# Attention over two head pairs at a time, in seven units of 128 keys, in place of four chunks of 112 keys for each pair

## The chip, the cores and the metric

The kernel runs on one core of one Trainium2 chip. The metric is the device time of one execution in microseconds; three runs of the kernel before gave 884.6, 885.2 and 886.6 us, so the median is 885.2 us.

## What is computed

The reference has three parts, one behind the other:

```python
# q, k, v: (4, 12, 448, 64)
scores = scale * q @ k.T - log(448)
attn   = 1 / (1 + exp(-scores))          # a sigmoid for each score, no sum over a row
x      = (attn @ v) -> (1792, 768)       # 4 batches of 448 tokens, 12 heads of 64
logits = x @ w_gate                      # 8 experts; each takes 224 tokens, the best logits first
x      = expert(x)                       # relu(x @ w1[e]) @ w2[e]
g      = s * relu(x @ w_in) ** 2 + b
out    = g @ w_out
```

Since the sigmoid has no sum over a row, each key contributes by itself: scores of some keys against all 448 queries, the sigmoid, and a product with those keys' rows of v that is added to the output.

## The kernel before

**Layout.** Two heads of 64 make a pair of 128 partitions; there are 4 batches of 6 pairs, 24 in all (`pairs`). Of each pair the kernel loads q and k, transposed, as 128 x 448 each (`load_qk`, L271), and v as 112 x 4 x 128 (`load_v`, L266).

**Scores.** `scores(n, c0, c1)` (L287) takes chunks of 112 keys of pair n. For a chunk the two heads j sit on the lower and the upper 64 rows of TensorE, each writes 112 keys x 448 queries to a PSUM bank of its own, and ScalarE makes one sigmoid of both (L304). From the third pair on q and k are split into a high part and a rest (`split_qk`, L278, on VectorE), and each head's product is made of three fp32r matmuls; the first two pairs (`PLAIN`) use fp32 matmuls on the raw tiles, which show as two instructions each in the trace. Three PSUM tiles (`psc`) of two banks each go round.

**Values.** `values(i)` (L308) multiplies the four chunks' sigmoids by v in fp32: the two heads sit on the two halves of 64 columns of TensorE, over 112 rows of keys, and add up in one bank `pv`. ScalarE copies the bank to `xT` (L321).

**Gate.** The logits of a batch are made from `xT`: `gate` (L323) puts pairs on four strips of 32 columns, four pairs first and the other two an iteration later; `gate_copy` takes them to SBUF, `gate_turn` (L335) turns them in an iteration of the next batch, and `prefs` (L348) makes ranks of them. The last batch leaves its last pair to `gate_last` (L343). `bracket` (L359) finds limits of the logits for the auction that follows.

**Order.** The order of work is written out by hand. Iteration i over the 24 pairs issues on SyncE's queue the loads of q and k of pair i+4 and of v of pair i+3; on VectorE the split of pair i+3; on TensorE values(i), the last two chunks of pair i+1 and the first two of pair i+2; then the gate's share. Each iteration ends with `CONV[i]` calls of `convert` (L159): VectorE turns one block of `w_in` or `w_out` from 8-byte words into floats in four or five instructions, SyncE's queue writes the block before out (`cv_out`, 384 KB) and then, when the raw tile is free, loads another (`cv_in`, 768 KB). SyncE's queue takes these in order, so a `cv_in` that waits for VectorE holds back the loads behind it. The raw q and k tiles have four buffers, the splits five and four (`wsp`, `wlp`).

After the loop come the transposes of `xT`, the auction, the gathers of tokens, the experts and the two layers; the change doesn't touch them.

Of the kernel before, what the change touches and what calls it, by code (L numbers as in the profile page):

```python
# [43 lines left out]
CONV = [1] * 8 + [2] + [1] * 7 + [2] + [1] * 5 + [0]  # L44
LATE = 8
PLAIN = 2
# [17 lines left out]
def tile_kernel(ctx, tc, qT, kT, v, wg, w1, w2, wi, wo, s2, b2, cst, out):  # L64
# [56 lines left out]
    qk = att.enter_context(tc.tile_pool(name="qk", bufs=4))  # L121
# [141 lines left out]
    raw_qk, two_qk, vt, attn, plg, lgs, pts = {}, {}, {}, {}, {}, {}, {}  # L263
# [14 lines left out]
    def split_qk(i):  # L278
        r = raw_qk.pop(i)
# [7 lines left out]
    def scores(n, c0, c1):  # L287
        if n >= len(pairs):
            return
        if c0 == 0:  # L290
            attn[n] = at.tile([CP, 2, NC, S], F32, name="attn")
        if n < PLAIN:
            terms = [(raw_qk[n], raw_qk[n])]
        else:
            h, lo = two_qk[n]
            terms = [(h, h), (lo, h), (h, lo)]
        for c in range(c0, c1):
            p = ps_s.tile([CP, 2, 512], F32, name="psc")
            for m, (kx, qx) in enumerate(terms):
                for j in range(2):  # L300
                    me = slice(j * D, (j + 1) * D)
                    T.matmul(p[:, j, :S], kx[me, 1, c * CP:(c + 1) * CP], qx[me, 0], start=(m == 0),  # L302
                             stop=(m == len(terms) - 1))
            A.activation(attn[n][:, :, c, :], p[:, :, :S], AF.Sigmoid, bias=nls[:CP], scale=1.0 / math.sqrt(D))  # L304
        if c1 == NC:
            (raw_qk if n < PLAIN else two_qk).pop(n)

    def values(i):  # L308
        a, v = attn.pop(i), vt.pop(i)
        pv = ps_v.tile([128, 512], F32, name="pv")  # L310
        for c in range(NC):
            for j in range(2):
                T.matmul(pv[j * 64:(j + 1) * 64, :S], v[:, c, j * D:(j + 1) * D], a[:, j, c, :],  # L313
                         start=(c == 0), stop=(c == NC - 1))
        b, p = pairs[i]
        xt = xT[:, p, b * S:(b + 1) * S]
        if i == len(pairs) - 1:
            A.copy(xt[:, :2 * CP], pv[:, :2 * CP])
            A.copy(xt[:, 2 * CP:], pv[:, 2 * CP:S])
        else:  # L320
            A.copy(xt, pv[:, :S])  # L321

    def gate(b, p0, p1, last):  # L323
        if p0 == 0:
            plg[b] = ps_l.tile([128, 512], F32, name="small")
# [9 lines left out]
    def gate_turn(b, stop):  # L335
        lg = lgs.pop(b)
        pt = ps_l.tile([128, 512], F32, name="small")
# [5 lines left out]
    def gate_last(b):  # L343
        for c in range(NC):
            T.matmul(pts[b][:, c], xT[:, NP - 1, b * S + c * CP:b * S + (c + 1) * CP], wgs[:, NP - 1, :E],
                     start=False, stop=(c == NC - 1))

    def prefs(b):  # L348
        V.tensor_copy(L[:, b * NC:(b + 1) * NC], pts.pop(b))
# [9 lines left out]
    def bracket(stage):  # L359
# [4 lines left out]
        elif stage == 1:  # L364
            pm = ps_l.tile([128, 512], F32, name="small")
            T.transpose(pm[:2, :CP], mm[:CP], ident[:CP, :CP])
            m2 = ep.tile([2, 1], F32, name="m2")
            V.tensor_reduce(m2, pm[:2, :CP], axis=AX.X, op=ALU.max)
            V.tensor_scalar(dg, ident[:2, :2], m2, None, op0=ALU.mult)
        else:  # L370
            pr = ps_l.tile([128, 512], F32, name="small")
            T.matmul(pr[:, :2], on[:2], dg, start=True, stop=True)
            V.tensor_copy(mm, pr[:, :2])
# [17 lines left out]
    keep_clock(WARM[0], ps_s.tile([CP, 2, 512], F32, name="psc")[:, 0])  # L391
# [4 lines left out]
    load_v(0)  # L396
    load_qk(1)
    nc.sync.dma_start(ct, cst)
    G.memset(wgs, 0.0)
    nc.sync.dma_start(wgs[:, :, :E], wg)  # L400
    load_v(1)
    load_qk(2)
    cv_in()
    load_qk(3)
    load_v(2)
    cv_in()
    cv_in()
    split_qk(2)
# [885 lines left out]
```

## Time and profile before

| | |
|---|---|
| median of three runs | 885.2 us |
| the profiled execution | 886.49 us, of it 884.7 us span |
| TensorE busy | 868.4 us (98%) |
| VectorE, ScalarE, GpSimd busy | 643.7, 520.1, 91.6 us |
| attention, from the first values to the last | 9.69 to 158.02 us |
| granted clock, mean | 0.993 |

Times within the profile are microseconds from the start of the span. "PE" is TensorE's matmuls, "PEld" its weight loads, "DVE" VectorE, "ACT" ScalarE, "POOL" GpSimd, "SPq" SyncE's queue of DMA issues. A matmul's end is modelled, so the spacing of starts tells more than the durations.

### The profile page before, as it was taken

The numbers are of one execution on the slowest core, as the hardware profiler recorded it, in microseconds if no ns is written. First come the engines' busy times: TensorE is split into PE (matmuls) and PEld (weight loads), VectorE is DVE, ScalarE is ACT, GpSimd is POOL, SyncE is SP. The second block draws the span as 40 slices with busy tenths as digits, with TensorE's granted clock in tenths as the row PEclk, the third lists the DMA queues.
The fourth block names the chain that finished last, engine by engine and source line by source line (L and its number), as shares of the span: only waits on it lengthen the run. The fifth ranks groups of instructions, "written<-read, shape, count | busy, mean of one in ns | idle before, by whom it ended". The sixth has DMA issues, their size and how long they took to land.

```text
span 884.7 us, 14248 instructions
## 1 busy us (share of the span) xinstructions
PE 868.4 (98%) x5226; PEld 749.3 (85%) x5226; DVE 643.7 (73%) x1114; ACT 520.1 (59%) x893; POOL 91.6 (10%) x150
## 2 busy tenths in 40 slices
PE   9999999889999999999999999999999999999997
PEld 4454544559999999999999999999998899999997
DVE  3987878556878677779778876867887666857681
ACT  6676767745765566643665546767766554645540
POOL 1000001323000000000255422000000000000003
PEclk9999999989999999999999999999999999999999
DMA  8989996666668686658899987675753333332313
GB/s 294 317 294 326 319 343 225 192 202 221 197 218 292 230 287 211 207 189 294 283 336 321 301 228 245 214 226 182 232 161 116 111 104 106 119 108 90 99 37 134
DMA packets 78122, 190.40 MB, mean 215 GB/s; under 512 B 9312, under 2 KB 31328, under 8 KB 77792
## 3 DMA queue, kind: packets, MB, share of 16 engines
q1 hardware_dynamic: 70144, 164.28, 56.6%
q0 software_dynamic: 7904, 25.17, 10.0%
q8 instruction: 42, 0.69, 0.3%
q14 instruction: 32, 0.26, 0.1%
HBM read 161.11 MB, written 42.47 MB: 230 GB/s over the span
## 4 chain that ended last, share of the span: by engine, by line
PE 94%; DVE 2%; ACT 1%; issue 1%; DMA 1%; POOL 0%; POOLq 0%; DVEq 0%; ACTq 0%
PE acc L727 16%; PE pv L313 9%; PE psc L302 8%; PE acc L728 8%; PE acc L1042 7%; PE acc L1039 7%; PE acc L1041 6%; PE acc L884 4%; PE acc L886 4%; PE acc L885 4%; PE acc L1148 4%; PE acc L1150 4%; PE acc L1149 4%; PE acc L753 1%; PE acc L754 1%; PE acc L755 1%
## 5 line engine op out<-in xcount | busy, mean ns | idle before, releaser
L244 ACT CAST wh<-raw 128x768 fp32r<-128x768 f32 (+1 forms) x248 | 201.2, 823 | 91.3 <-issue 68.1
L254 DVE TENSOR_TENSOR wl<-raw,wh 128x768 fp32r<-128x768 f32 (+1 forms) x244 | 225.8, 937 | 18.3 <-PE acc L1041 11.3
L727 PE MATMUL acc<-u,wh 128*128 128x448 f32 x384 | 120.8, 374 | 0.0
L728 PE MATMUL acc<-u,wl 128*128 128x224 f32 x384 | 101.6, 265 | 0.1
L727 PE MATMUL acc<-x,wh 128*128 128x448 f32 x288 | 94.8, 384 | 0.8 <-DVE x L721 0.8
L304 ACT ACTIVATE attn<-psc,nls 112x896 f32<-112x896 f32 x96 | 88.8, 1009 | 9.8 <-PE psc L302 9.8
L313 PE MATMUL pv<-attn,vt 112*64 112x448 f32 x384 | 77.5, 545 | 0.0
L728 PE MATMUL acc<-x,wl 128*128 128x224 f32 x288 | 76.8, 267 | 0.0
L727 PEld LDWEIGHTS acc<-u,wh 128*128 128x128 f32 x384 | 72.0, 188 | 5.3
L728 PEld LDWEIGHTS acc<-u,wl 128*128 128x128 f32 x384 | 73.3, 191 | 0.4 <-DVE wl L254 0.4
L884 PE MATMUL acc<-y,wh 128*128 128x448 f32 x192 | 70.9, 369 | 0.0
L886 PE MATMUL acc<-y,wl 128*128 128x448 f32 x192 | 70.2, 366 | 0.0
L885 PE MATMUL acc<-y,wh 128*128 128x448 f32 x192 | 70.2, 366 | 0.0
L313 PEld LDWEIGHTS pv<-attn,vt 112*64 112x64 f32 x384 | 25.4, 136 | 42.9 <-issue 36.1
L732 ACT COPY tmp<-acc 128x224 f32<-128x224 f32 x96 | 32.9, 343 | 48.7 <-PE acc L728 48.0
L727 PEld LDWEIGHTS acc<-x,wh 128*128 128x128 f32 x288 | 54.9, 191 | 4.9 <-issue 0.9
L1042 PE MATMUL acc<-wh,as 128*128 128x384 f32 x168 | 56.1, 334 | 0.0
L1041 PE MATMUL acc<-wl,as 128*128 128x384 f32 x168 | 56.1, 334 | 0.0
L1039 PE MATMUL acc<-wh,as 128*128 128x384 f32 x168 | 56.1, 334 | 0.0
L728 PEld LDWEIGHTS acc<-x,wl 128*128 128x128 f32 x288 | 55.7, 194 | 0.0
L733 DVE TENSOR_TENSOR tmp<-acc,tmp 128x224 f32<-128x224 f32 x78 | 30.1, 385 | 26.6 <-ACT tmp L732 26.1
L618 POOL DMA_INDIRECT xr<-xs,idx x16 | 16.6, 1036 | 264.4 <-PE px L718 252.1
(336 smaller groups left out, 1987.3 us busy)
## 6 DMA issues: line engine op xcount, KB each, us to landing
raw<-in_w_dram SPq DMA_DIRECT2D x128, 384.0 KB, 3.8
raw<-nw SPq DMA_DIRECT2D x64, 384.0 KB, 3.6
craw<-in_wi_dram SPq DMA_DIRECT2D x16, 768.0 KB, 7.1
raw<-mx SPq DMA_DIRECT2D x32, 384.0 KB, 5.0
nw<-co SPq DMA_DIRECT2D x24, 384.0 KB, 6.9
craw<-in_wo_dram SPq DMA_DIRECT2D x8, 768.0 KB, 6.4
ra<-in_wo_dram SPq DMA_DIRECT2D x8, 768.0 KB, 5.8
hs<-nw POOLq DMA_DIRECT2D x16, 384.0 KB, 9.6
```

What stands on the lines that cost most here:

```text
L244: A.copy(h, r)
L254: eng.tensor_sub(lo, r, h.bitcast(F32))
L304: A.activation(attn[n][:, :, c, :], p[:, :, :S], AF.Sigmoid, bias=nls[:CP], scale=1.0 / math.sqrt(D))
L313: T.matmul(pv[j * 64:(j + 1) * 64, :S], v[:, c, j * D:(j + 1) * D], a[:, j, c, :], start=(c == 0), stop=(c == NC - 1))
L727: T.matmul(p[:, :2 * CAP], wh, src[:, k].rearrange("p a s -> p (a s)"), start=(k == 0), stop=False)
L728: T.matmul(p[:, :CAP], wl, src[:, k, 0], start=False, stop=(k == n - 1))
L884: T.matmul(p, wh, src[:, k, 0], start=first, stop=False)
L885: T.matmul(p, wh, src[:, k, 1], start=False, stop=False)
L886: T.matmul(p, wl, src[:, k, 0], start=False, stop=last)
L1039: T.matmul(acc, hi, wh[:, cols], start=(opens[j] and u == 0 and c == 0), stop=False, skip_group_check=True)
L1041: T.matmul(acc, hi, wl[:, cols], start=False, stop=False, skip_group_check=True)
L1042: T.matmul(acc, lo, wh[:, cols], start=False, stop=(u == 3 and c == 1), skip_group_check=True)
```

## The change

Two neighbouring pairs, 2q and 2q+1, are taken together, in 12 steps (`NQ`). Of each pair's 448 keys the first 384 (`HD`) make three units of 128 keys; the 64 keys that are left of both pairs make one more unit, so there are seven: units 0 to 2 are the first pair's, 3 the two rests, 4 to 6 the second pair's. In unit 3 the scores of pair n go to the partitions n*64 to n*64+63, so that head j and pair n take the quarter of TensorE with row half j and column half n; it is made in plain fp32 from the raw tiles. In the values of unit 3 pair n is on row half n and head j on column half j, and the results end in the two banks of the two pairs. A step has two halves: values of units 0 to 2, then scores of the next step's units 0 to 2; values of units 3 to 6, then scores of the next step's units 3 to 6. v comes in one load for two pairs, 128 x 7 x 128. The raw tiles get five buffers and are held until unit 3 has used them. The gate's own PSUM bank goes; small results take tiles of the `psc` ring, and copies of them are ScalarE's. `gate` takes six pairs at once in the next batch's first step, and the last batch leaves two pairs to `gate_last`. `CONV` has a second 2 at one place less.

```diff
-CONV = [1] * 8 + [2] + [1] * 7 + [2] + [1] * 5 + [0]
+CONV = [1] * 8 + [2] + [1] * 14 + [0]
-PLAIN = 2
+PLAIN = 1
+NQ = B * NP // 2
+HD = 3 * 128
-    qk = att.enter_context(tc.tile_pool(name="qk", bufs=4))
+    qk = att.enter_context(tc.tile_pool(name="qk", bufs=5))
-    ps_v = att.enter_context(tc.tile_pool(name="ps_v", bufs=1, space=PSUM))
-    ps_l = att.enter_context(tc.tile_pool(name="ps_l", bufs=1, space=PSUM))
+    ps_v = att.enter_context(tc.tile_pool(name="ps_v", bufs=2, space=PSUM))
-    def load_v(i):
-        b, p = pairs[i]
-        vt[i] = vp.tile([CP, NC, 128], F32, name="vt", bufs=5)
-        nc.sync.dma_start(vt[i], v[b, p])
+    def load_v(q):
+        vt[q] = vp.tile([128, 7, 128], F32, name="vt", bufs=3)
+        nc.sync.dma_start(vt[q], v[q // 3, q % 3])
+    def small_psum():
+        return ps_s.tile([128, 2, 512], F32, name="psc")[:, 0]
+    def scores(q, units):
+        if q >= NQ:
             return
+        for r in units:
+            p = ps_s.tile([128, 2, 512], F32, name="psc")
+            if r == 3:
+                work = [(2 * q + n, slice(HD, S), slice(n * 64, n * 64 + 64)) for n in range(2)]
+            else:
+                c = r % 4
+                work = [(2 * q + r // 4, slice(c * 128, (c + 1) * 128), slice(0, 128))]
+            plain = q < PLAIN or r == 3
+            n_terms = 1 if plain else 3
+            for m in range(n_terms):
                 for j in range(2):
                     me = slice(j * D, (j + 1) * D)
+                    for n, keys, rows in work:
+                        if plain:
+                            kx = qx = raw_qk[n]
+                        else:
+                            h, lo = two_qk[n]
+                            kx, qx = ((h, h), (lo, h), (h, lo))[m]
+                        T.matmul(p[rows, j, :S], kx[me, 1, keys], qx[me, 0], start=(m == 0),
+                                 stop=(m == n_terms - 1), skip_group_check=True)
+            attn[q, r] = at.tile([128, 2, S], F32, name="attn", bufs=7)
+            A.activation(attn[q, r], p[:, :, :S], AF.Sigmoid, bias=nls, scale=1.0 / math.sqrt(D))
+    def values(q, block):
+        v = vt[q]
+        pvs[q, block] = pv = ps_v.tile([128, 512], F32, name="pv")
+        if block:
+            a = attn.pop((q, 3))
+            for n in range(2):
+                rows = slice(n * 64, n * 64 + 64)
+                for j in range(2):
+                    T.matmul(pvs[q, n][j * 64:(j + 1) * 64, :S], v[rows, 3, j * D:(j + 1) * D], a[rows, j],
+                             start=(n == 1), stop=(n == 0), skip_group_check=True)
+            done(q, 0)
+        for c in range(3):
+            a = attn.pop((q, 4 * block + c))
             for j in range(2):
+                T.matmul(pv[j * 64:(j + 1) * 64, :S], v[:, 4 * block + c, j * D:(j + 1) * D], a[:, j],
+                         start=(block == 0 and c == 0), stop=(block == 1 and c == 2), skip_group_check=True)
+        if block:
+            done(q, 1)
     def gate_last(b):
+        for p in (NP - 2, NP - 1):
+            for c in range(NC):
+                T.matmul(pts[b][:, c], xT[:, p, ...], wgs[:, p, :E],
+                         start=False, stop=(p == NP - 1 and c == NC - 1))
...
+    scores(0, range(7))
+    load_qk(4)
...
+    split_qk(2)
+    split_qk(3)
+    for q in range(NQ):
+        b, t = divmod(q, 3)
+        closing = b == B - 1
+        for n in (2 * q + 5, 2 * q + 6):
+            if n < 2 * NQ:
+                load_qk(n)
+        if q + 2 < NQ:
+            load_v(q + 2)
+        for half in range(2):
+            if q + 2 < NQ:
+                split_qk(2 * q + 4 + half)
+            values(q, half)
+            if t == 0 and b:
+                if half:
+                    gate_turn(b - 1, True)
+                    prefs(b - 1)
+                else:
+                    gate(b - 1, 0, NP, NP)
+                    gate_copy(b - 1)
+            if closing and (t == 1 or t + half == 1):
+                bracket(2 * t + half - 1)
+            if closing and t == 2 and not half:
+                gate(b, 0, NP - 2, NP - 2)
                 gate_copy(b)
+            scores(q + 1, range(3, 7) if half else range(3))
+            n = 2 * (NQ - q) - half
+            if 2 < n <= 6:
+                w_dma()
+            for _ in range({4: 1, 3: 1, 2: 2}.get(n, 0)):
+                w_high()
+                w_low(G)
+            for _ in range(CONV[2 * q + half]):
                 convert()
```

## Rows read from the trace of the kernel before

**Rows 1.** The page: the chain that ended last, by line.

```profile
PE acc L727 16%; PE pv L313 9%; PE psc L302 8%; PE acc L728 8%; PE acc L1042 7%; PE acc L1039 7%; PE acc L1041 6%; PE acc L884 4%; PE acc L886 4%; PE acc L885 4%; PE acc L1148 4%; PE acc L1150 4%; PE acc L1149 4%; PE acc L753 1%; PE acc L754 1%; PE acc L755 1%
```

**Rows 2.** Windows of attention: busy by engine (instructions), clock, DMA share, GB/s.

```profile
20.00:140.00 120.00, 120.00 (x818) 60.36 (x816) 99.28 (x145) 81.41 (x98) 0.00 (x0) 1.00 0.94 317
```

**Rows 3.** Timeline of TensorE over one iteration: start, duration, what, instructions merged.

```profile
27.62 3.23 PE L313 MATMUL pv<-attn,vt 112*64 112x448 f32 x16
30.78 0.46 PE L302 MATMUL psc<-wh 64*112 64x448 f32 x2
31.07 0.37 PE L302 MATMUL psc<-wh,wl 64*112 64x448 f32 x2
...
32.50 0.37 PE L302 MATMUL psc<-wl,wh 64*112 64x448 f32 x2
32.75 0.46 PE L302 MATMUL psc<-wh 64*112 64x448 f32 x2
...
33.24 0.37 PE L302 MATMUL psc<-wl,wh 64*112 64x448 f32 x2
33.54 0.60 PE L313 MATMUL pv<-attn,vt 112*64 112x448 f32 x2
```

**Rows 4.** Timeline of TensorE at the gate: four strips, two strips, and the turn.

```profile
39.47 0.96 PE L328 MATMUL small<-xT,wgs 128*32 128x448 f32 x8
40.36 3.23 PE L313 MATMUL pv<-attn,vt 112*64 112x448 f32 x16
...
46.28 0.95 PE L328 MATMUL small<-xT,wgs 128*32 128x448 f32 x4
47.16 0.60 PE L313 MATMUL pv<-attn,vt 112*64 112x448 f32 x2
...
53.09 0.95 PE L340 MATMUL small<-ct,lg 128*112 128x8 f32 x8
53.97 0.60 PE L313 MATMUL pv<-attn,vt 112*64 112x448 f32 x2
```

**Rows 5.** Groups of ScalarE, 20 to 140 us: count, busy, mean ns, idle before.

```profile
L304 ACT ACTIVATE attn<-psc,nls 112x896 f32<-112x896 f32 x76 | 70.3, 1008 | 4.9 <-PE psc L302 4.9
L321 ACT COPY xT<-pv 128x448 f32<-128x448 f32 x19 | 10.1, 534 | 33.9 <-PE pv L313 33.9
```

**Rows 6.** Timeline of VectorE: a split's start and its conversion's last instruction.

```profile
102.93 0.63 DVE L283 CAST wh<-rqk 128x896 fp32r<-128x896 f32 x1 [0.56 <-DMA rqk<-in_qT_dram]
...
106.53 0.96 DVE L157 CUSTOM_DVE_ANT_0 co<-co,cb__1250 128x1536 uint16<-128x1536 uint16 x1
```

**Rows 7.** DMA from 2 to 141.4 us: the sum, and issues with size and time to landing.

```profile
DMA packets 17615, 44.43 MB, mean 319 GB/s; under 512 B 2944, under 2 KB 9068, under 8 KB 17604
...
craw<-in_wi_dram SPq DMA_DIRECT2D x16, 768.0 KB, 7.1
nw<-co SPq DMA_DIRECT2D x22, 384.0 KB, 7.0
...
rqk<-in_kT_dram SPq DMA_DIRECT2D x23, 224.0 KB, 6.8
```

**Rows 8.** Timeline of the start: the six first sigmoids, the first values, the first split.

```profile
5.89 5.49 ACT L304 ACTIVATE attn<-psc,nls 112x896 f32<-112x896 f32 x6 [3.67 <-PE psc L302]
...
9.69 3.23 PE L313 MATMUL pv<-attn,vt 112*64 112x448 f32 x16
...
13.06 1.09 DVE L284 TENSOR_TENSOR wl<-rqk,wh 128x896 fp32r<-128x896 f32 x1
```

**Rows 9.** Timeline of TensorE behind the last values.

```profile
158.02 0.95 PE L340 MATMUL small<-ct,lg 128*112 128x8 f32 x8
158.82 0.93 PE L345 MATMUL small<-wgs,xT 128*112 128x8 f32 x8
```

**Rows 10.** Timeline: the last split's last instruction, and the first scores made of it.

```profile
142.06 1.09 DVE L284 TENSOR_TENSOR wl<-rqk,wh 128x896 fp32r<-128x896 f32 x1
...
147.57 0.46 PE L302 MATMUL psc<-wh 64*112 64x448 f32 x2
```

More of the change, by code (lines that the diff above doesn't have):

```diff
@@ L278, in split_qk @@
     def split_qk(i):
-        r = raw_qk.pop(i)
+        r = raw_qk[i]
         h = wsp.tile([128, 2 * S], F32R, name="wh")
@@ L316, in values, with done @@
+    def done(q, n):
+        b, p = pairs[2 * q + n]
+        pv = pvs.pop((q, n))
         xt = xT[:, p, b * S:(b + 1) * S]
-        if i == len(pairs) - 1:
+        if (q, n) == (NQ - 1, 1):
             A.copy(xt[:, :2 * CP], pv[:, :2 * CP])
@@ L324, in gate @@
         if p0 == 0:
-            plg[b] = ps_l.tile([128, 512], F32, name="small")
+            plg[b] = small_psum()
         for p in range(p0, p1):
@@ L336, in gate_turn @@
         lg = lgs.pop(b)
-        pt = ps_l.tile([128, 512], F32, name="small")
+        pt = small_psum()
         pts[b] = pt[:CP, :NC * E].rearrange("p (c e) -> p c e", e=E)
@@ L343, in gate_last @@
     def gate_last(b):
-        for c in range(NC):
-            T.matmul(pts[b][:, c], xT[:, NP - 1, b * S + c * CP:b * S + (c + 1) * CP], wgs[:, NP - 1, :E],
-                     start=False, stop=(c == NC - 1))
+        for p in (NP - 2, NP - 1):
+            for c in range(NC):
+                T.matmul(pts[b][:, c], xT[:, p, b * S + c * CP:b * S + (c + 1) * CP], wgs[:, p, :E],
+                         start=False, stop=(p == NP - 1 and c == NC - 1))
     def prefs(b):
-        V.tensor_copy(L[:, b * NC:(b + 1) * NC], pts.pop(b))
+        A.copy(L[:, b * NC:(b + 1) * NC], pts.pop(b))
         lb = L[:, b * NC:(b + 1) * NC]
@@ L389, in keep_clock @@
             T.matmul(p, zero[:, :CP], zero, start=True, stop=True)
-    keep_clock(WARM[0], ps_s.tile([CP, 2, 512], F32, name="psc")[:, 0])
+    keep_clock(WARM[0], small_psum()[:CP])
     warm = ep.tile([1, 1], F32, name="warm")
@@ L395, in tile_kernel @@
     load_qk(0)
-    load_v(0)
     load_qk(1)
     nc.sync.dma_start(ct, cst)
+    load_v(0)
     G.memset(wgs, 0.0)
     nc.sync.dma_start(wgs[:, :, :E], wg)
+    load_qk(2)
+    load_qk(3)
+    cv_in()
     load_v(1)
[L402 to L405, printed above, removed]
     cv_in()
     cv_in()
-    split_qk(2)
-    scores(0, 0, NC)
-    scores(1, 0, 2)
+    scores(0, range(7))
+    load_qk(4)
     nc.sync.dma_start(sb2[:, 0:1], s2.partition_broadcast(128))
@@ L423, in tile_kernel @@
     identb, rival, samee, prev, tri, nege = (cb[:, n] for n in range(6))
-    N = len(pairs)
-    for i in range(N):
-        b, p = pairs[i]
-        if i + 4 < N:
-            load_qk(i + 4)
-        if i + 3 < N:
-            load_v(i + 3)
-        if i + 3 < N:
-            split_qk(i + 3)
-        values(i)
-        scores(i + 1, 2, NC)
-        scores(i + 2, 0, 2)
-        if p == 0 and b:
-            gate_turn(b - 1, True)
-            prefs(b - 1)
-        elif p == 4:
-            gate(b, 0, 4 if b < B - 1 else 5, 6 if b < B - 1 else 5)
-            if b == B - 1:
-                gate_copy(b)
-        elif p == 5 and b < B - 1:
-            gate(b, 4, 6, 6)
-            gate_copy(b)
-        if b == B - 1 and 1 <= p <= 3:
-            bracket(p - 1)
-        if N - 6 <= i < N - 2:
-            w_dma()
-        for _ in range((1, 1, 2, 0)[i - N] if i >= N - 4 else 0):
-            w_high()
-            w_low(G)
-        if i < N - 1:
-            for _ in range(CONV[i]):
+    split_qk(2)
[23 more added lines that the diff above has]
+                gate(b, 0, NP - 2, NP - 2)
+                gate_copy(b)
+            scores(q + 1, range(3, 7) if half else range(3))
[6 more added lines that the diff above has]
+            for _ in range(CONV[2 * q + half]):
                 convert()
```

47 lines of the change are left out of this document (17 added, 30 removed).

## The prediction

> **What bounds the kernel now.** I read the chain that ended last first: values (L313) and scores (L302) hold 17% of the span, all as TensorE [rows 1]. The windows of attention show TensorE busy without a break at full clock, VectorE 83%, ScalarE 68%, and the DMA engines at 0.94 [rows 2]: TensorE bounds this stage, and DMA stands close behind it. The timeline of an iteration gives the prices. The eight fp32 slots of a pair's values (two instructions side by side in each) take 3.16 us from 27.62 to the first scores, and scores take 2.76 us from 30.78 to the next values, together 5.92 [rows 3]. Three iterations of each batch are longer by a gate's share of 0.88 to 0.89 [rows 4].
>
> **Prices.** An fp32 slot s and the cost c of changing from one use of the array to another follow from two rows: values are 8s + c = 3.16, and the gate with four strips, which is two slots, 2s + c = 0.89. So s = 0.378 and c = 0.13 us. An fp32r slot is 0.204 (31.07 to 32.50, seven slots). The first slot of a run of scores takes 0.29, 0.09 more; leaving for values costs 0.10 (33.24 to 33.54 is 0.30); and a wait for a PSUM tile before the fourth chunk with its restart costs 0.05 + 0.09 = 0.14 [rows 3]. Check: 12 x 0.204 + 0.09 + 0.10 + 0.14 = 2.78, shown 2.76.
>
> **One step of the new order**, two pairs, before 2 x 5.92 = 11.84:
> - values of three units: 6s + c = 2.40
> - scores of three units: 9 x 0.204 + 0.19 = 2.03
> - values of the rests, if the four quarters run side by side: 2s + c = 0.89; values of three units 2.40
> - scores of the rests in fp32, the same 0.89; three units 2.03, and I leave the PSUM wait in, 0.14
>
> The sum is 10.78, so 1.06 less. The two more changes of the array's use are in it, at c each. A unit of 128 keys costs the same as a chunk of 112, since a slot streams 448 queries either way. Weight loads get longer by 128/112, but run under the slots.
>
> The gate: before 0.89 + 0.88 + 0.88 = 2.65 us a batch; after, six pairs in one go are 4s + c = 1.64 and the turn 0.88, 2.52. In the last batch four pairs (0.89) take the place of five (4s + c = 1.64). What moves to `gate_last` is on the path: its four products have the shape of the turn's four, which took 0.80 us (158.02 to 158.82), and they become eight, so 0.80 more at the end [rows 9]. The copies of the last values lie under the turn.
>
> **The start.** Six sigmoids came at a pitch of 5.49/6 = 0.92 us and values began at 9.69 [rows 8]. Now seven units come ahead of them, paced by ScalarE, so values begin near 10.6. The first three units end at 13.0. The next scores need the third pair's split. That pair's q and k stand behind the same 2.5 MB in SyncE's queue as before (two pairs, v of two pairs, the constants), so I leave the split's end at 14.15 [rows 8]: a wait of 1.15 us.
>
> **Sum.** Before, by these prices: 24 x 3.16 for values; 21 x 2.76 for scores, 2.92 for the first iteration's (two fp32 chunks, 4s, and six fp32r slots and 0.19) and 1.41 for the last's two chunks; 3 x 2.65 + 1.64 for the gate, and 0.5, an estimate that is the same on both sides, for the two products of `bracket`: 148.2, so 9.69 + 148.2 = 157.9; the trace has 158.02 [rows 8, 9]. After: 12 x (2.40 + 3.29) + 11 x (2.03 + 3.06) + 3 x 2.52 + 0.89 + 0.5 + 1.15 = 134.4, so 10.6 + 134.4 = 145.0. The difference is 12.9, less 0.80 at the end: 12.1 us. What follows attention is a chain that the change doesn't touch, so I pass it on whole. The profiled execution took 886.5, which gives 874.4; the median of three is 885.2, 1.3 below it, which gives **873.1 us**.
>
> **What must stay hidden.** ScalarE: seven sigmoids and two copies a step, 7 x 0.92 + 2 x 0.53 = 7.5 of 10.78 [rows 5, 8]; the three small copies it takes over stand ahead of sigmoids that wait for TensorE behind the same small product, so they cost nothing; if they were not covered, some 0.3 us each, ten in all. The fourth unit of the second half uses a PSUM tile whose sigmoid ended about when TensorE gets there. VectorE: a split and a conversion take 4.56 us [rows 6], 9.1 a step. The longer v loads move the same bytes.
>
> DMA is the one to count. The order of SyncE's queue up to the last pair's q and k: before, 24 pairs of q and k at 0.459 MB, 22 of v at 0.229, 0.68 of constants, 24 raw blocks at 0.786, 20 written blocks and one weight at 0.393, 43.9 MB. After, with one doubled conversion less ahead of it and the split one conversion earlier: 11.0 + 11 x 0.459 + 0.68 + 22 x 0.786 + 18 x 0.393 = 41.1 MB. At the rate of before, 319 GB/s [rows 7], 41.1 MB from 2 us on have landed at 130.9, and the split ends at 132.6. Scores need it at 145.0 less the last step's values and gate (2.40 + 0.89 + 3.29) and the three units made of it (2.17), 136.2, so 3.6 us are spare; before it was 147.57 - 143.15 = 4.4 [rows 10]. The same count for the pairs that come second in their loads' steps leaves 2.6 us for pair 19, where it is tightest of those I worked out (33.6 MB, 109.0 against 111.6). So hidden, by a margin that a lower rate by 3% uses up.
>
> **Rivals.**
> (a) *The quarters don't run four at a time.* No row shows the array split in rows and columns at once. For it: heads on two row halves run side by side in scores, on two column halves in values [rows 3], and the gate's four strips with eight fp32 instructions take 0.89, the same as two strips with four, 0.88 [rows 4]; so four tiles of fp32 run at once, its two instructions included. Against it: each fp32 product is two instructions in the same quarter, and if the second holds up the next quarters, two of the four run at a time, and a rest takes two slots more, 0.756. With 12 values and 11 scores that is 17.4 us: 873.1 + 17.4 = **890.5**, slower. If they run one by one it is six slots more, 52 us, 925. It decides from 12.1/23 = 0.53 us a rest unit on.
> The Trainium skill, "TensorE: Matmul & The Clock Gate", in Part 3 (packing small matmuls), says both that tiles split in rows and columns overlap almost fully and that matmuls start and end strictly in program order; by the first the time is the sum's, by the second, with the instructions of a product next to each other, this rival's. The gate's row agrees with the first; for quarters no run here shows either.
> (b) *The loads come too late.* SyncE's queue takes a `cv_in` only when VectorE is through with a raw block, VectorE waits for q and k, and a load took 7 us to land [rows 7]; that loop kept just ahead of TensorE before. Raw tiles are now held until unit 3 of the scores, which is some 2 us ahead of the step in which the next loads stand, so loads can't run ahead more than that. If the loop gets no faster at all, the last split ends at 143.15 as before [rows 10], 6.9 us later than needed, and of 12.1 us 5.2 are left: **880.0**. With only the two conversions fewer ahead of it (2 x 2.9) it ends at 137.4, 1.2 late, 874.3. What speaks against the worse end: the DMA share of 0.94 leaves 6% of 130 us, 8 us, if more is always under way.
> (c) *More is gained:* the PSUM wait (0.14 x 11) and the wait at the start (1.15) both vanish, the slots' changes cost nothing in column mode (0.13 x 23): 5.7 us more, **867.4**.
> (d) *The gain is given back behind attention*, in the auction's waits or a clock that falls at another place: within 0.2%, **885**. Nothing in the rows speaks for it, since that stage begins when attention ends.
>
> **Chances.** The sum's case, 870 to 877: 0.60. Late loads, 877 to 883: 0.18. (c), below 870: 0.08. (a), above 887: 0.11. (d): 0.03. Within 0.2%, 1.8 us, is about what a measurement of this kernel can't tell from no change: faster 0.85, same 0.04, slower 0.11. The range takes the sum's case, most of (b) and the nearer half of (c): 869 to 882.5; the likeliest case's own is 870 to 877.
>
> **What the profile after would show.** Right: the last values end near 145; a step from values to values 10.8 us, 13.3 with the gate; a rest unit 0.9 us, its first four matmuls starting within some 0.03 us of each other; VectorE's splits ahead of the scores that use them. Wrong: quarter units of 1.6 us or more (a), or TensorE idle ahead of scores until a split (b), most likely in the second halves of steps, where the pair came last in its load. The prediction fails most surely if the rests cost more than 0.5 us above the 0.89 that I give them.

## The result, and the profile after

The changed kernel took 877.42 us (median of five executions, 874.08 to 879.17) against 884.6 (882.9 to 886.6) before: a ratio of 0.9907, 95% interval 0.9883 to 0.9931. The interval lies below 1, so it is faster, by 7.2 us where 12.1 were forecast. The profiled execution took 876.09, with a span of 874.3 and a granted clock of 0.992.

The attention stage did what was forecast. The page's chain by line and the windows answer to [rows 1, 2]:

```profile
PE acc L757 15%; PE acc L758 7%; PE acc L1069 7%; PE acc L1072 7%; PE acc L1071 7%; PE psc L310 6%; PE pv L334 5%; PE acc L914 4%; PE acc L915 4%; PE acc L916 4%; PE acc L1178 4%; PE acc L1180 4%; PE acc L1179 4%; PE acc L783 1%; PE acc L784 1%; PE acc L785 1%
```

```profile
20.00:140.00 120.00, 119.69 (x857) 57.54 (x853) 106.86 (x161) 81.74 (x104) 1.81 (x1) 1.00 0.93 333
```

TensorE is still busy throughout, yet scores and values hold only 11% of the chain in place of 17%. The stage didn't shrink that much: the chain leaves TensorE at 118 us. The chain in order of time (start, duration) goes on with the load of pair 23's queries and then with VectorE's work, up to the end of the attention:

```profile
115.61 1.63 PE psc L354 x12
118.21 7.58 DMA rqk<-in_qT_dram
...
134.07 2.51 DVE co L157
...
145.77 2.45 DVE co L157
150.45 1.45 PE px L508 x12
```

In the kernel before it stays with TensorE to the end of the attention. So VectorE is the engine to look at next: 106.86 us of 120 at work in place of 99.28. What it did in the rest stands in the views of waits for the same window, after and before (total, times, longest), and the first of these waits after in VectorE's timeline:

```profile
DVE wh L282 <- DMA rqk<-in_qT_dram: 15.1, 8, 6.0
```

```profile
DVE wh L283 <- DMA rqk<-in_qT_dram: 16.1, 13, 3.9
```

```profile
20.23 0.63 DVE L282 CAST wh<-rqk 128x896 fp32r<-128x896 f32 x1 [5.99 <-DMA rqk<-in_qT_dram]
```

All but 0.23 us of that first wait lie ahead of the window, which begins at 20 us; so after the change 9.4 us of the 120 are waits for loads. With the 106.86 this leaves 3.8 us, most of it gaps of under 0.15 us. Before, 99.28 and 16.1 left 4.6. So VectorE was at work or waiting for a load nearly all the time in both kernels, and waited less after the change. These waits are partly its own doing: the loads stand behind `cv_in` on SyncE's queue, and up to 160 us `cv_in` waited 55.1 us for VectorE (61.9 before).

TensorE's timeline (start, duration) shows a step, the gate and its turn, and what stands behind the last values [rows 3, 4, 9]:

```profile
27.42 2.48 PE L334 MATMUL pv<-attn,vt 128*64 128x448 f32 x12
29.83 0.98 PE L310 MATMUL psc<-rqk 64*64 64x448 f32 x8
30.74 0.47 PE L310 MATMUL psc<-wh 64*128 64x448 f32 x2
...
32.83 2.48 PE L334 MATMUL pv<-attn,vt 128*64 128x448 f32 x12
...
37.26 0.98 PE L328 MATMUL pv<-attn,vt 64*64 64x448 f32 x8
38.17 2.48 PE L334 MATMUL pv<-attn,vt 128*64 128x448 f32 x12
...
43.58 2.48 PE L334 MATMUL pv<-attn,vt 128*64 128x448 f32 x12
45.99 1.70 PE L354 MATMUL psc<-xT,wgs 128*32 128x448 f32 x12
47.62 0.47 PE L310 MATMUL psc<-wh 64*128 64x448 f32 x2
...
52.96 0.95 PE L366 MATMUL psc<-ct,lg 128*112 128x8 f32 x8
...
129.17 0.26 PE L393 MATMUL psc<-ident,mm 112*2 112x112 f32 x1 [0.31 <-DVE mm L390]
...
142.22 2.48 PE L334 MATMUL pv<-attn,vt 128*64 128x448 f32 x12
144.62 0.95 PE L366 MATMUL psc<-ct,lg 128*112 128x8 f32 x8
145.43 1.72 PE L372 MATMUL psc<-wgs,xT 128*112 128x8 f32 x16
```

A step is 43.58 - 32.83 = 10.75 us. The rests take 38.17 - 37.26 = 0.91 us as values and 30.74 - 29.83 = 0.91 as scores, and the gate 1.63. The last values end at 144.62, 13.4 us earlier than before [rows 9]. But the span is only 10.4 us shorter, so 3.0 us are given back behind the last values; the doubled `gate_last` makes the last preferences 0.8 later. One small wait is new: at 129.17 TensorE stands 0.31 us for VectorE, in the bracket. The kernel before had room there. Its bracket's last reduction and the transpose that needs it, and the same reduction in the changed kernel:

```profile
137.19 0.24 DVE L363 TENSOR_REDUCE mm<-L 112x1 f32<-112x96 f32 x1
...
142.25 0.26 PE L366 MATMUL small<-ident,mm 112*2 112x112 f32 x1
```

```profile
128.79 0.24 DVE L390 TENSOR_REDUCE mm<-L 112x1 f32<-112x96 f32 x1
```

Before, the reduction ended 4.8 us ahead of the transpose; after, at 129.03, it is what the transpose waits for. The change's own order took that room: before, the preferences came in iteration 18 and the reductions in iteration 19 behind the split of pair 22; after, both come in half step 19, behind the split of pair 23. That leads to the cause. The start [rows 8], the last split and the scores made of it [rows 10], from the timeline of all engines:

```profile
11.31 2.48 PE L334 MATMUL pv<-attn,vt 128*64 128x448 f32 x12
11.48 1.09 DVE L283 TENSOR_TENSOR wl<-rqk,wh 128x896 fp32r<-128x896 f32 x1
...
13.72 0.47 PE L310 MATMUL psc<-wh 64*128 64x448 f32 x2
...
126.61 1.09 DVE L283 TENSOR_TENSOR wl<-rqk,wh 128x896 fp32r<-128x896 f32 x1
...
135.95 0.47 PE L310 MATMUL psc<-wh 64*128 64x448 f32 x2
```

No scores wait for a split at either end: the first have 1.2 us to spare, the last 8.2.

### The profile page after: what moved, and what is told of

It is laid out like the page before. It is cut to its first block, busy times and chain, and to the rows that moved or that the text cites. A ratio compares the mean times of both kernels' runs of the same rounds, so it can differ in the third digit from the quotient of the medians.

```text
span 874.3 us, 14225 instructions
## 1 busy us (share of the span) xinstructions
PE 857.2 (98%) x5188; PEld 740.3 (85%) x5188; DVE 645.3 (74%) x1109; ACT 509.9 (58%) x887; POOL 92.9 (11%) x150
## 3 DMA queue, kind: packets, MB, share of 16 engines
q0 software_dynamic: 7904, 25.17, 10.2%
## 4 chain that ended last, share of the span: by engine, by line
PE 89%; DVE 5%; DMA 2%; ACT 1%; issue 1%; POOL 0%; POOLq 0%; DVEq 0%; ACTq 0%; SPq 0%
PE acc L757 15%; PE acc L758 7%; PE acc L1069 7%; PE acc L1072 7%; PE acc L1071 7%; PE psc L310 6%; PE pv L334 5%; PE acc L914 4%; PE acc L915 4%; PE acc L916 4%; PE acc L1178 4%; PE acc L1180 4%; PE acc L1179 4%; PE acc L783 1%; PE acc L784 1%; PE acc L785 1%
## 5 line engine op out<-in xcount | busy, mean ns | idle before, releaser
L313 ACT ACTIVATE attn<-psc,nls 128x896 f32<-128x896 f32 x84 | 78.1, 1009 | 23.5 <-PE psc L310 23.4
L334 PE MATMUL pv<-attn,vt 128*64 128x448 f32 x288 | 59.4, 548 | 0.0
L334 PEld LDWEIGHTS pv<-attn,vt 128*64 128x64 f32 x288 | 18.5, 136 | 34.8 <-issue 33.9
L648 POOL DMA_INDIRECT xr<-xs,idx x16 | 16.1, 1008 | 264.9 <-PE px L748 251.9
```

The costliest lines, as they stand in the source:

```text
L313: A.activation(attn[q, r], p[:, :, :S], AF.Sigmoid, bias=nls, scale=1.0 / math.sqrt(D))
L334: T.matmul(pv[j * 64:(j + 1) * 64, :S], v[:, 4 * block + c, j * D:(j + 1) * D], a[:, j], start=(block == 0 and c == 0), stop=(block == 1 a ...
```

## The experiments

The theory that came out of the first trace: VectorE waits for loads, and its order carries that to TensorE or past the attention. Its rivals: the loads are late for the scores themselves, or the rest is lost behind the attention whatever happens in it. From `swap` on these carry the letters A, B and C of its expectation. Every ratio is to the kernel before on the same chip.

**The changed kernel again**, `again`, without an edit.

> The changed kernel once more, nothing edited, for a second trace and more times. In the first trace attention ended 13.4 us earlier, and from the first copy of the last values to the end of the span it took 729.6 us against 726.5 before; 1.2 of these 3 us are at once behind the last values (gate_last), the rest at single late DMA landings. Theory 1 (TensorE's slots set attention, what is lost behind it is chance from run to run): attention again ends at 144.7 within 0.3 us, the stretch behind it comes out somewhere between 727 and 733, and the median gain is 8 to 11 us. Theory 2 (the earlier start costs something fixed behind attention, by the clock or the DMA queue): the stretch again takes 3 us or more longer, with the same places late (the weights read back near 244 us), and the gain is 7 to 8.

878.59 us (875.86 to 880.95, six executions), ratio 0.9916, interval 0.9893 to 0.9939. The profiled execution took 879.97, and its attention ends 4 us later than in the first trace. The timelines of VectorE and TensorE show why:

```profile
128.31 0.63 DVE L282 CAST wh<-rqk 128x896 fp32r<-128x896 f32 x1 [2.77 <-DMA rqk<-in_qT_dram]
129.04 1.09 DVE L283 TENSOR_TENSOR wl<-rqk,wh 128x896 fp32r<-128x896 f32 x1
130.05 0.42 DVE L380 TENSOR_TENSOR ge<-L 112x256 f32<-112x256 f32 x1
...
131.21 0.24 DVE L390 TENSOR_REDUCE mm<-L 112x1 f32<-112x96 f32 x1
```

```profile
131.60 0.31 PE L393 MATMUL psc<-ident,mm 112*2 112x112 f32 x1 [3.46 <-DVE mm L390]
131.84 0.74 PE L310 MATMUL psc<-wh 64*128 64x448 f32 x2
...
135.33 0.98 PE L328 MATMUL pv<-attn,vt 64*64 64x448 f32 x8
```

Read it from the load: the split of pair 23 waits 2.77 us for it; the preferences and the bracket's reductions (L389, L390) stand behind the split in VectorE's order; and TensorE's transpose of these reductions (L393) stands ahead of scores that need nothing of them. TensorE waits 3.46 us, and the scores behind it take 3.49 us rather than 2.1, at a granted clock of 0.51 (131.6 to 135.1), the 1.2 GHz level. The scores that are made of this split came only at 139.87, 9.7 us after its end. So in this run the loads are late for the bracket, not for the scores. Neither theory holds as it was written: the attention didn't end at 144.7 again; behind it the stretch is 2.95 us longer than before once more, but the read-back of weights that is late at 244.16 us in the first trace is not on the chain here.

**The order of the rests**, `order`: values of the rests behind those of the blocks, next to the scores of the rests.

```diff
+        for c in range(3):
+            ...
         if block:
             a = attn.pop((q, 3))
             ...
-        for c in range(3):
-            ...
```

> In the second half of a step the values of the rests come last, right ahead of the scores of the rests, so that the array stays in quarters from the one to the other; nothing else. By the price of a change of the array's use, 0.13 us, one of six changes a step goes: 11 x 0.13 = 1.4 us less attention, a step of 10.62 in place of 10.75, and the last values end near 143.3. If the price is not for the change but for the switch of operands (another tile, another wait), the step stays at 10.75. If the copies of both pairs, which now come together, hold up ScalarE's sigmoids, the step gets longer by up to the 0.53 us of a copy.

878.5 us, ratio 0.9913 (0.9892 to 0.9933). TensorE's timeline shows the effect in the step, and the wait again:

```profile
38.43 0.98 PE L333 MATMUL pv<-attn,vt 64*64 64x448 f32 x8
39.24 0.93 PE L310 MATMUL psc<-rqk 64*64 64x448 f32 x8
...
130.95 0.34 PE L392 MATMUL psc<-ident,mm 112*2 112x112 f32 x1 [4.15 <-DVE mm L389]
```

The rests take 0.81 and 0.86 us, a step 10.59 rather than 10.75 (25.44 to 36.03). The Trainium skill, "TensorEngine Tiling (Array Packing)", Key Properties, says that a change of the tiling mode drains the array. The trace agrees that a change costs something: with one change fewer the two rests take 0.10 and 0.05 us less, 0.16 a step where 0.13 was expected. But the wait is 4.15 us here, and the median is that of the change: this gain on TensorE doesn't reach the end.

**The rests apart**, `apart`: the two pairs' quarters computed at different times, two at once.

```diff
         if block:
-            a = attn.pop((q, 3))
-            ...
+            rest(0)
         for c in range(3):
             ...
         if block:
-            done(q, 1)
+            rest(1)
```

(and the same in `scores`, with a chunk between the two halves of the rest)

> The quarter units are taken apart: the rests of the two pairs are computed at different times (values: the first pair's rest, three units, the second pair's rest; scores: the first pair's rest, a unit, the second pair's rest), so two quarters run at a time in place of four. If the gain rests on four quarters side by side, each rest costs two slots and a change more, 2 x 0.376 + 0.13 = 0.88 us, 12 in values and 12 in scores (the first of them under ScalarE's pace at the start), 20 us in all: some 897, slower than before the change by 1.4%. If the quarters gave little (the pairs' units of 128 keys being what pays), the time stays within 5 us of the changed kernel.

904.11 us, ratio 1.0203 (1.0179 to 1.0228), 25.5 us above the changed kernel. A rest of one pair alone takes as long as both together:

```profile
29.61 0.97 PE L339 MATMUL pv<-attn,vt 64*64 64x448 f32 x4
30.51 2.48 PE L348 MATMUL pv<-attn,vt 128*64 128x448 f32 x12
```

0.90 us for two quarters with four instructions, 0.91 for four quarters with eight. So four quarters do run side by side, and that carries the whole change: without it the kernel is slower than before. The 897 expected were too few: 4.2 of the 7 us beyond are twelve waits of the scores for ScalarE that the change doesn't have. In this run a step takes TensorE 2.4 us more, and the bracket's transpose doesn't wait.

**More loads**, `load`: an unused read of 384 KB in each half of the first ten steps, 7.9 MB in all.

```diff
             ...
             for _ in range(CONV[2 * q + half]):
                 convert()
+            if q < 10:
+                extra = vp.tile([128, KD, 128], F32, name="extra", bufs=2)
+                nc.sync.dma_start(extra, w1[q % E, half])
```

> A read of 384 KB of weights that nobody uses is added to SyncE's queue in each half of the first ten steps, 7.9 MB in 20 loads, to find out how near the loads stand to being the bound. In the changed kernel's trace the last split ended 8.2 us ahead of the scores made of it, while DMA moved 337 to 361 GB/s from 40 to 120 us. By rate, 49 MB are ahead of the last pair's landing in place of 41.1; at 345 GB/s that is 142 + 2 + 1.7 us against 136 needed: attention ends some 10 us later, with TensorE waiting for splits. If the loads were far from bounding, nothing changes; if they bounded already, all 7.9 MB show, 23 us.

890.98 us, ratio 1.0062 (1.0037 to 1.0087), 12.4 above the changed kernel, near the 10 expected. But most of it isn't at the scores, where it was expected. In the profile VectorE waits 29.1 us for queries and keys up to 150 us (19.2 in `again`), and TensorE's wait at the transpose grows to 9.07; six runs of scores wait for their splits, 3.0 us in all (timeline and waits of TensorE):

```profile
142.22 0.35 PE L393 MATMUL psc<-ident,mm 112*2 112x112 f32 x1 [9.07 <-DVE mm L390]
```

```profile
PE psc L310 <- DVE wl L283: 3.0, 6, 0.6
```

**The wait taken away in four ways.** `swap` issues the split of pair 23 behind the bracket's reductions on VectorE; `later` issues the bracket's second and third stage half a step later; `swap_load` and `swap_order` join `swap` with the edits above.

```diff
-            if q + 2 < NQ:
+            if q + 2 < NQ and (q, half) != (9, 1):
                 split_qk(2 * q + 4 + half)
             ...
             if closing and (t == 1 or t + half == 1):
                 bracket(2 * t + half - 1)
+            if (q, half) == (9, 1):
+                split_qk(23)
```

```diff
-            if closing and (t == 1 or t + half == 1):
-                bracket(2 * t + half - 1)
+            if closing and (2 * t + half) in (1, 3, 4):
+                bracket({1: 0, 3: 1, 4: 2}[2 * t + half])
```

> The changed kernel, except that the last split of queries and keys (pair 23) is issued on VectorE behind the bracket's first stage rather than ahead of the copies of preferences, so that TensorE's transpose of the bracket's second stage depends on nothing that waits for the loads of pair 23. Theory A (the loads' lateness reaches TensorE only through VectorE's order, at this transpose): the transpose waits under 0.5 us in the profile, the scores of pair 23 still find their split done (it ended 9.7 us ahead of need in the run called again, so some 8 us are left), the scores at half clock right behind the transpose are gone, the copies of the last values come at 144.3 to 145.5 us, and the median is 3 to 4 us below the changed kernel's 878.5 of this chip: 874 to 876, ratio to before about 0.988. Theory B (the loads are late for TensorE wherever they are first needed): the wait comes back at the scores of pairs 22 and 23, the copies of the last values come at 147 to 149, and the median stays at 878. Theory C (the stall is real but what it costs is given back behind the attention, where weights are awaited): the copies come at about 145 and the median stays at 877 to 879.

> The changed kernel with the split where it is, but the second and third stage of the bracket issued half a step (some 5 us of TensorE's work) later each. Theory A: the wait of the transpose for VectorE (0.4 to 4.2 us in the runs so far) is under these 5 us and goes in nearly every execution; copies of the last values at 144.3 to 145.5, median 874 to 876 as with the exchange of the order on VectorE. Theory B: TensorE waits instead at scores; 147 to 149 and 878. If only the exchange of the order on VectorE helps and this one doesn't, it is the time VectorE loses that counts and not TensorE's place.

> The exchange on VectorE together with the extra unused read of 384 KB in each half of the first ten steps, which alone cost 12.4 us over the changed kernel, 9.1 of them in the wait of the bracket's transpose. Theory A: most of the 9.1 us goes, since the scores of pair 23 had 8 to 10 us to spare without the extra reads; what remains is a wait at the scores of pair 22 and 23 of 0 to 4 us and the 2 to 3 us of small waits in earlier steps; copies of the last values at 147 to 152, median 879 to 884. Theory B: the extra reads bind at the scores as much as at the transpose: copies at 158 to 161, median 889 to 892.

> The exchange on VectorE together with the values of the rests moved behind those of the blocks, right ahead of the scores of the rests, so that the array goes from whole tiles to quarters and back once in a half step and not twice. By theory A and the run called order (steps of 10.59 rather than 10.75): 12 times 0.1 to 0.16, or 1.2 to 2 us, below the exchange alone: copies of the last values at 142.5 to 144, median 872.5 to 874.5. If the quarters' order is worth nothing once the stall is gone: the same as the exchange alone.

Medians: `swap` 875.06 (ratio 0.9891, 0.9872 to 0.9909), `later` 874.88 (0.9893, 0.9866 to 0.9919), `swap_order` 875.96 (0.9901, 0.9885 to 0.9918), `swap_load` 886.15 (1.0003, 0.998 to 1.0025). The medians of `swap` and `later` lie in theory A's 874 to 876. In `later`, which gives the bracket half a step back, TensorE doesn't wait at all up to the last values, and from the first values to the copies of the last it takes 132.95 us. In `swap` 1.09 and 1.21 us are left where theory A had under 0.5: VectorE is late at the bracket without this split too, and the second wait comes from a small product on VectorE that takes 1.48 us (0.22 in `again`) while GpSimd splits weights, a matter of the last section (TensorE's and VectorE's timelines):

```profile
130.68 0.26 PE L393 MATMUL psc<-ident,mm 112*2 112x112 f32 x1 [1.09 <-DVE mm L390]
...
137.49 0.35 PE L401 MATMUL psc<-dg,on 2*128 2x2 f32 x2 [1.21 <-DVE dg L398]
```

```profile
135.86 1.48 DVE L398 TENSOR_SCALAR dg<-ident,m 2x2 f32<-2x2 f32 x1
```

`swap_order` missed its 872.5 to 874.5: its stage is 1.8 us shorter than that of `swap`, as expected, its median isn't lower. With the extra loads the wait shrinks from 9.07 to 3.6 us and TensorE's stage by 6.5 (149.91 to 143.40), as theory A has it in kind. But the wait isn't gone, scores wait as they did in `load` (those begun at 70.14 and 77.49 take 2.95 and 2.92 us rather than 2.1), and 886.15 lies between the forecasts of A and B: with so much more to load, each holds in part. In `swap` no scores waited for a split.

The profiled execution of `later` (875.02) is still only 1.1 us ahead of the change's first: behind the attention VectorE is late again. Its timeline in `later`, where ScalarE copied the last preferences at 146.62, and in the kernel before:

```profile
147.67 0.96 DVE L157 CUSTOM_DVE_ANT_0 co<-co,cb__1686 128x1536 uint16<-128x1536 uint16 x1
148.55 0.42 DVE L380 TENSOR_TENSOR ge<-L 112x256 f32<-112x256 f32 x1
```

```profile
159.79 0.19 DVE L349 COPY L<-small 112x32 f32<-112x32 f32 x1 [5.01 <-PE small L345]
160.02 0.42 DVE L353 TENSOR_TENSOR ge<-L 112x256 f32<-112x256 f32 x1
```

Before, the ranking followed its data by 0.23 us, and VectorE had been idle for 5 us. Now the last conversion stands ahead of it, and the ranking comes 1.9 us after its data.

**Can it be had together?** `later_order` joins `later` with the order of the rests; `later_conv` joins it with a list in which the last conversion comes one half step earlier and half step 13 has two; `later_order_conv` has all three; `latest` has them too, with the bracket's third stage behind the attention.

```diff
-CONV = [1] * 8 + [2] + [1] * 14 + [0]
+CONV = [1] * 8 + [2] + [1] * 4 + [2] + [1] * 8 + [0, 0]
```

```diff
+    bracket(2)
     gate_turn(B - 1, False)
```

> The later bracket together with the values of the rests moved behind those of the blocks. In the runs so far first values to the copies of the last values took 133.0 us with the later bracket alone, 138.1 with the other order and the stall, 133.6 with the other order and 0.6 us of stall. If the order's gain of 0.16 us in each half step where the quarters are adjacent adds to the later bracket's: 133.0 less 9 times 0.16, so 131.3 to 131.8, and a median 1 to 2 us below the later bracket's (about 873.5 where that gave 874.9). If not: 133.0 and the same median.

> The later bracket, and the list of conversions ends one half step earlier: the last conversion comes in half step 21 rather than 22 of 24 and an earlier half step (13) has two. Before the change the last conversion's last instruction began 4.3 us ahead of the copies of the last values, with the later bracket 3.5 us behind them, and VectorE began the ranking of preferences 4.37 us behind the copies rather than 1.88. Theory A (part of what is given back behind the attention is this conversion in VectorE's order): ranking at 2.6 to 2.7 behind the copies, the first price column 1.3 to 1.7 us nearer to them than 6.0, median 1 to 1.7 us below the later bracket's, if nothing behind takes it back. Theory B (what is given back is given back by loads or by the granted clock): the ranking comes earlier but the end does not; median unchanged, the last values to the end 729 as before. The two conversions of half step 13 put 3 us of work ahead of the splits; these have 8 us to spare, so no wait at scores is expected.

> All three together: the sum of the two, 2.3 to 3.4 us below the later bracket's median (871.5 to 872.6 where that gave 874.9); ratio to before about 0.985. If the clock or the loads decide behind the attention: 873 to 874.

> The three edits of later_order_conv, with the bracket's third stage issued behind the attention, ahead of the last turn of the gate, rather than in the last step: its matmul waits for two small VectorE operations that stood behind two conversions (of 3 to 5 us each) in VectorE's order, and cost TensorE 3.4 to 3.5 us in three of the last four runs. Theory A (what TensorE loses at the end of the attention is its two waits for VectorE's order in the bracket, and nothing else there waits for VectorE or for loads): no wait over 0.5 us from the first values to the last, 131.3 to 131.8 us from the first values to the copies of the last values (137.3 in later_order, 140.2 in later_order_conv), the half-clock stretch ahead of the last values gone, 728 to 729 from the copies to the end, as the bracket's matmul adds some 0.35; median 872 to 873.5, ratio to before 0.985 to 0.987. Theory B (VectorE is the bound of the last third itself, and takes back elsewhere what is not waited for in the bracket): waits at scores or at PSUM of 2 to 4 us come in the place of the bracket's, 134 to 137 us, the median stays at 876 to 878. Theory C (given back behind the attention): 131.5 us there, but over 731 from the copies to the end, median at 875.

876.71 (0.9902, 0.9876 to 0.9928), 878.03 (0.9913, 0.9881 to 0.9945), 878.5 (0.9918, 0.9896 to 0.9941) and 876.73 (0.99, 0.9883 to 0.9916). All four sums failed: none came out better than `later` alone. The stages from the profiles, in us (the kernel before, for comparison: 148.45, 1.88, 726.55, 154.79):

| kernel | first values to copies of the last | copies to ranking | copies to the end | VectorE's last conversion ends at |
|---|---|---|---|---|
| after, first trace | 133.43 | 3.40 | 729.55 | 148.22 |
| `again` | 138.01 | 2.66 | 729.50 | 147.90 |
| `order` | 138.09 | 2.25 | 728.91 | 149.14 |
| `swap` | 135.40 | 4.36 | 728.76 | 151.93 |
| `later` | 132.95 | 4.37 | 729.04 | 148.63 |
| `swap_order` | 133.64 | 4.09 | 729.01 | 148.60 |
| `later_order` | 137.33 | 2.68 | 726.32 | 151.19 |
| `later_conv` | 139.14 | 2.66 | 726.56 | 146.56 |
| `later_order_conv` | 140.17 | 2.44 | 728.54 | 145.80 |
| `latest` | 135.15 | 4.73 | 730.55 | 149.20 |

Where TensorE's stage is shorter (133 to 135.4), the ranking is later; where the ranking follows at once, TensorE's stage is 137 to 140. The last column hardly moves: VectorE ends its conversions at 146 to 152 in every version of the table, 3 to 9 us ahead of the kernel before. In `later_order`, `later_conv` and `later_order_conv` the matmul of the bracket's third stage waits 3.4 to 3.5 us, where the transpose of the second had. In `latest` the two wait 0.46 and 1.13, one run of scores waits 0.85 for its split (103.46, behind the half step with two conversions), and the ranking is the latest of all. VectorE and TensorE in `later_order`:

```profile
134.41 2.48 DVE L157 CUSTOM_DVE_ANT_0 co<-co,cb__1529 128x1536 uint16<-128x1536 uint16 x1
...
138.76 2.44 DVE L157 CUSTOM_DVE_ANT_0 co<-co,cb__1578 128x1536 uint16<-128x1536 uint16 x1
141.12 0.25 DVE L396 TENSOR_REDUCE m<-mt 2x1 f32<-2x112 f32 x1
```

```profile
141.77 0.35 PE L400 MATMUL psc<-dg,on 2*128 2x2 f32 x2 [3.38 <-DVE dg L397]
```

The copy that `m` reads was there at 133.9; two conversions stood ahead of it. What the move was to save came back one stage on. But 3.0 of the 3.38 us are longer instructions: the last ones of these two conversions take 2.48 and 2.44 us, each beside a split of weights on GpSimd, where they take 0.96 otherwise. `later_conv` and `later_order_conv` have the same (2.44 to 2.56, twice); in `later` neither met GpSimd, and TensorE didn't wait:

```profile
132.12 0.96 DVE L157 CUSTOM_DVE_ANT_0 co<-co,cb__1578 128x1536 uint16<-128x1536 uint16 x1
```

Whether the edits bring these meetings about or they differ from execution to execution no run separates. The numbers of `latest` are those of its theory B (135.15 us and 876.73), and VectorE was on the chain in the first trace too. That VectorE bounds the end of the attention nearly as tightly as TensorE fits all of this; it isn't shown by a run that takes work from VectorE.

## Why the prediction was right, and what it missed

**The prices held.** A step 10.78 forecast, 10.75 measured; a rest 0.89 and 0.91; the gate 1.64 and 1.63, its turn 0.88 and 0.88, the last gate 0.89 and 0.89 (140.42 to 141.31). The first values came at 11.31 in the first trace and at 10.2 to 12.1 in the others (10.6 forecast). The wait of 1.15 us at the start didn't come: the third pair's split ended at 11.48 + 1.09 = 12.57 rather than 14.15. The last values ended at 144.62, forecast 145.0. ScalarE stayed hidden, with 81.74 us of 120. The weight loads of scores got longer by less than 128/112 (171 to 184 ns in the mean), those of values not at all (136); nothing hung on it.

**Rival (a) fell**, by the first four matmuls of a rest starting within 0.02 us (37.257 to 37.277), by its 0.91 us, and by `apart`, where a rest with two quarters at a time takes 0.90 and the kernel took 904.

**The step that failed** stands under "what must stay hidden": "VectorE: a split and a conversion take 4.56 us, 9.1 a step". Against a step of 10.78 that looked like room, but it counts busy time alone, and nobody asked what stands behind VectorE's waits for loads, or how far ahead of its use each small thing is made. The sum of work and waits would not have told it: the kernel before had as little left over, and TensorE never waited for VectorE there. What differed is the order: the bracket's reductions had 4.8 us to spare before and stand behind the last split now. The count of loads went to the scores: 3.6 us to spare forecast, 8.2 measured, from the split's end at 126.61 + 1.09 to 135.95, since the queues moved 340 GB/s up to 126 us where 319 were put in [rows 7]. The bracket's two products had 0.5 us, "an estimate that is the same on both sides"; in the seven traces with the bracket in its place and the rests together they held TensorE for 0.3 to 9.1 us, and not at all in `apart`, where TensorE is slower. So rival (b) had half of the mechanism, VectorE waiting for loads, and a fair size (880.0 or 874.3), but the wrong consumer: the bracket, not the scores. In the first trace that cost 0.31 us, in `again` 3.46.

**The second miss** is "I pass it on whole", and with it that nothing spoke for rival (d). From the copies of the last values to the end took 726.55 us before and 728.8 to 729.6 in the first trace, `again`, `order`, `swap` and `later`. The 0.8 of `gate_last` was priced right: the preferences are copied 2.44 us behind the first of these copies in place of 1.66. Another 0 to 1.7 up to the ranking is the last conversion ahead of it, which this change's own list put into half step 22 of 24 where the kernel before had its last in iteration 21. But the ranking doesn't settle the end: `again` and `later_conv` have it equally soon (2.66 us behind the copies), and the end comes 729.50 and 726.56 us behind them. The rest differs from trace to trace: a stretch at the lower clock under the first transposes in `later` (0.58 from 146 to 149), a read-back of weights that lands late in the first trace. That part stays open.

**The sum of the misses.** The first trace is 10.4 us shorter than that of before, where 12.1 were forecast: 0.5 more from the attention, 2.2 less behind it. The median of before in this measurement, 884.6, stands 1.9 us below its profiled execution, that of after 1.3 above (877.42 against 876.09), another 3.2; that makes 7.2. The trace of `again`, with 3.46 us of wait and 1.4 of half clock, shows what a slower execution can look like; that every one of them has this cause isn't shown. The recorded range held the result because it took in most of rival (b): 877.42 lies just outside the 870 to 877 of the sum's own case, in the band that was given to late loads with a chance of 0.18. The attention's own end, within 0.4 us, is the sum's; the total owes something to luck, since what was lost stands elsewhere than where the prediction put it.

**A better version?** `later` and `swap` are the fastest measured, 10.0 and 9.9 us below before on their chip where the change is 7.1 to 7.2 below on its own. The intervals of the ratios overlap, so the 3 us between them aren't proven; the change's first trace, with 0.31 us of wait, has a stage only 0.5 us longer than that of `later`.

## What to carry to other kernels

When the engine that bounds a stage is made faster, go through the order of each of the others: whatever the fast engine needs from one stands behind everything that waits there, however small the thing itself is. Read for each such thing how long ahead of its use it was made before the change (4.8 us here), and ask what of that the new order keeps. A one-instruction dependency (a transpose of a few maxima) cost up to 4.15 us here, while the large transfers that had been counted had 8 to spare. Don't take the sum of an engine's work and its waits for loads for a sign of a new bound unless the kernel before shows a smaller one; and look whether a wait lies within the window that it is counted in. If several reorderings each cure one wait and the end doesn't move, suspect the engine behind them, and test it by taking work from it.

## What was not expected of the hardware

With each of the seven waits of TensorE of over 3 us at the bracket (3.38 to 9.07) its granted clock fell to the lower level, 1.2 GHz, during the wait or within some 1 us behind it; with the waits of 0.31, 1.09 and 1.21 it didn't. The scores behind the first, in `again`, took 3.49 us rather than 2.1, so that wait cost 1.4 us more than itself.

A conversion's last instruction on VectorE takes 0.96 us alone and 2.4 to 2.6 where a split of weights is already running on GpSimd, as in `later_order` (GpSimd's timeline, beside VectorE's instruction at 134.41 shown above):

```profile
132.95 3.13 POOL L254 TENSOR_TENSOR wl<-raw,wh 128x768 fp32r<-128x768 f32 x1 [122.31 <-ACT wh L244]
```

The Trainium skill, "SBUF — State Buffer", section "SBUF: two separate sides", says that these two engines share a pair of ports as an exclusive lock, held for a whole instruction. The trace agrees: VectorE's instruction ends at 136.89, 0.81 us behind GpSimd's end at 136.08, nearly its own length. In `swap` VectorE's began first, at 143.28, by 0.1 us; it took 0.96 and GpSimd's 2.55. These clashes fell into the end of the attention, where TensorE waits for VectorE.
